# Loading the first pair's q and k into both partition halves, head by head on two queues, and making the router's constants later

## The chip, the cores and the metric

The kernel runs on one core of one Trainium2 chip. The metric is the device time of one execution in microseconds. A core has five engines that run their own instruction streams in order and wait for each other by semaphores: TensorE (PE, matmuls; PEld is its weight load), VectorE (DVE), ScalarE (ACT), GpSimd (POOL) and SyncE (SP), which here issues most of the DMAs; ScalarE can issue DMAs as well, from a queue of its own. Data lie in SBUF, in 128 partitions; TensorE writes to PSUM.

## What is computed

Attention over 8 batches and 8 heads with q pooled by two, then a mixture of experts with one expert for each of the 4608 rows:

```
q, k, v: (8, 8, 1152, 64) float32
q_pool = q.reshape(B, H, S // 2, 2, D).mean(axis=3)
scores = (1 / sqrt(D)) * q_pool @ k.transpose(0, 1, 3, 2)
attn   = softmax(scores)                 # row maximum subtracted
x      = (attn @ v) -> (4608, 512)
logits = x @ w_gate ; e = argmax(logits) ; gate = softmax(logits)[e]
out    = gate * sigmoid(x @ w_output_gate)[e] * (relu(x @ w1[e]) @ w2[e])
```

Everything is kept near float32 precision. A value is split into a high part (a cast to fp32r, or to fp16 for probabilities and v) and a low part (value minus high part), and a product is made of matmuls of these parts.

## The kernel before

**Pairs and tiles.** The heads are worked on in 32 pairs (one batch, two heads; `prep(n, table)` for pair n). A head has 64 dimensions, so a pair's q and k come as 128 partitions: head 0 in partitions 0 to 63, head 1 in 64 to 127. `qp` is q with its two rows to be pooled, `kpf` is k, `vp` is v. Matmuls need another layout: `ka[:, h]` holds head h's high part of k in both halves of the partitions, `qa` holds head h's high part of q in partitions 0 to 63 and its low part in 64 to 127, `kb` the low part of k and `qb` the high part of q in partitions 0 to 63; rows 64 to 67 of `kb` and `qb` carry constants and the row maxima. One matmul of `ka` with `qa` and one of `kb` with `qb` make three of the four products. `kp` (low part of k, both heads in their own halves) and `qd` serve the one query tile in which rows of both heads meet.

**How the layout is made.** `lk` loads q and k, two DMAs of 576 KB. `kh` casts k to `xk` (ACT), `qsum` adds the two rows of q (POOL), `qh` casts it to `xq` (ACT), `kl` and `ql` subtract for the low parts `kp` and `yq` (POOL), `qd` copies two corners (POOL). Then `dk`, `dq` and `dl` copy the parts from SBUF to SBUF into both halves: four DMAs for `ka`, two for `qa` and two for `qb` (from `xq`), two for `qa` and two for `kb` (from `yq` and `kp`). All twelve are issued by SP. `lv` loads v, `amax`, `gmax` and `scale` find its scale (ACT, a PE matmul over all partitions, DVE, POOL, DVE), and `vh`, `vs` and `vl` split it.

**Stages of a pair.** `mgen` makes the row maxima: 27 chunks for each pair, for each two or three matmuls into one of three PSUM banks (`mp`) and a reduction of DVE (`pm`). After the fifth query tile and after the last, `rows` transposes the maxima, DVE splits them into `mr`, and two small DMAs from ACT's queue (`qb<-mr`) write them into `qb`, rows 66 and 67. `scores` makes 18 steps of scores (`sps`), each with two exponentials on ACT and a subtraction on POOL or DVE; the second matmul of a step reads `qb`, so it needs the maxima. `av` multiplies by v, and `logits` and `router` choose the expert. After all pairs `Moe.run` does the experts.

**What sets the order.** PE, DVE, ACT and POOL run in the order in which the code records instructions. A table gives each step of `prep` a place in a grid of slots; the grid has 32 lead-in steps before the first score step. Pair 0 and pair 1 used `PREP0`, the others `PREP`. SP issues its DMAs in the recorded order as well. The DMAs of both queues share eight semaphores, so a DMA may also wait until the eighth before it has landed. `consts` makes the router's constants: it loads the router's weights (`wf`, 32 KB), splits them into `wgt` on ACT and DVE, and fills small tables on POOL; `init(0)` writes one row of zeros to memory and fills `di`. Both are recorded at lead-in step `1 - SLEAD + INIT`, so `INIT = 12` puts them 20 steps ahead of the first score step. The first matmul that reads `wgt` starts at 88.8 us.

Of the kernel before, what the change touches and what calls it, by code (L numbers as in the profile page):

```python
# [8 lines left out]
F32 = mybir.dt.float32  # L9
F32R = mybir.dt.float32r  # L10
# [5 lines left out]
ALU = mybir.AluOpType  # L16
# [7 lines left out]
PREP0 = ((0, 'lk'), (12, 'kh', 0), (13, 'kh', 1), (12, 'qsum'), (15, 'kl'), (18, 'dk', 0), (19, 'dk', 1), (21, 'qh'), (26, 'ql'), (26, 'dq', 0), (27, 'dq', 1), (29, 'qd'), (32, 'dl', 0), (33, 'dl', 1),  # L24
        (53, 'lv'), (71, 'amax', 0), (74, 'amax', 1), (81, 'gmax'), (82, 'scale', 0), (85, 'scale', 1), (90, 'scale', 2), (93, 'vh', 0), (93, 'vs', 0), (96, 'vh', 1), (97, 'vl', 0), (100, 'vs', 1), (104, 'vl', 1))
PREP = ((0, 'lk'), (12, 'kh', 0), (12, 'qsum'), (17, 'kh', 1), (18, 'kl'), (18, 'dk', 0), (19, 'dk', 1), (22, 'qh'), (24, 'dq', 0), (25, 'dq', 1), (26, 'ql'), (29, 'qd'), (30, 'dl', 0), (32, 'dl', 1),
        (63, 'lv'), (82, 'amax', 0), (88, 'amax', 1), (93, 'gmax'), (94, 'scale', 0), (95, 'scale', 1), (99, 'scale', 2), (100, 'vh', 0), (101, 'vs', 0), (103, 'vl', 0), (107, 'vh', 1), (107, 'vs', 1), (110, 'vl', 1))
BURST = {0: 2, 2: 2, 4: 2, 6: 2, 8: 1, 10: 2, 12: 2, 14: 2, 16: 3}
PLP = (1, 3, 7, 9, 13, 15)
PLPL = (1, 3, 5, 7, 9, 11, 13, 15, 17)  # L30
IMM = 0
INIT = 12
KPB = 2
ND = 18
NS = 3
# [27 lines left out]
def attention(tc, qT, kT, vL, wg, keep, xrows, idscr, cum, pairs, setup, scat, init):  # L63
    nc = tc.nc
    nb = len(pairs) // 4
    with ExitStack() as ctx:
        def pool(name, bufs=1, **kw):
            return ctx.enter_context(tc.tile_pool(name=name, bufs=bufs, **kw))
# [4 lines left out]
        ld = pool("a_ld")  # L73
        sq = pool("a_sq")
# [8 lines left out]
        def psum(hold=False, name="tp"):  # L83

            while len(held) == 3:
                pop() if fill else pendv.pop(0)()
            k = next(i for i in banks if i not in held)
            free(k)
            if hold:
                held.add(k)  # L90
            x = ps_m.tile([128, 512], F32, name=name, tag=f"mp{k}")
            return (x, k) if hold else x

        def free(k):
# [12 lines left out]
        QDs = [ep.tile([128, 128], F32R, name=f"qd{i}") for i in range(2)]  # L107
# [12 lines left out]
        def dmaf(o, i, q=nc.sync):  # L120
            q.dma_start(out=o.bitcast(F32), in_=i.bitcast(F32))

        def prep(n, table):

            p = pairs[n]
            b, hp = p
            ka, kb, qa, qb, vt = KAs[n % 3], KBs[n % 3], QAs[n % 3], QBs[n % 3], VTs[n % 2]
            sc = sm.tile([128, 2], F32, name="sc", bufs=4)
            states[n] = dict(ka=ka, kb=kb, qa=qa, qb=qb, vt=vt, sc=sc, p=p, n=n, qd=QDs[n % 2])
            kp = ld.tile([128, S], F32R, name=f"kp{n}", tag="kp", bufs=KPB)  # L130
            kpf = ld.tile([128, S], F32, name="kpf")
            states[n]['kp'] = kp
            qp = ld.tile([128, 2, NQ], F32, name="qp")
            vp = ld.tile([128, 2 * NC, 64], F32, name="vp")
            xk = sq.tile([128, S], F32R, name=f"xk{n}", tag="xk")
            yq = sq.tile([128, NQ], F32R, name="yq")
            qs = yq.bitcast(F32)
            xq = sq.tile([128, NQ], F32R, name="xq")
            am = sm.tile([128, 2], F32, name="am")
            ex = sm.tile([128, 2], U32, name="ex")  # L140
            inv2 = sm.tile([128, 2], F32, name="inv2")
            gm = []

            def lk():
                nc.sync.dma_start(out=qp, in_=qT[b, hp].rearrange("p (t n) -> p t n", t=2))
                nc.sync.dma_start(out=kpf, in_=kT[b, hp])

            def lv():
                nc.sync.dma_start(out=vp, in_=vL[b, hp].rearrange("p (c d) -> p c d", d=64))

            def kh(i):
                z = slice(i * NQ, i * NQ + NQ)
                nc.scalar.copy(out=xk[:, z], in_=kpf[:, z])

            def kl():
                nc.gpsimd.tensor_tensor(out=kp, in0=kpf, in1=xk.bitcast(F32), op=ALU.subtract)

            def qsum():
                nc.gpsimd.tensor_tensor(out=qs, in0=qp[:, 0], in1=qp[:, 1], op=ALU.add)

            def qh():
                nc.scalar.copy(out=xq, in_=qs)

            def ql():
                nc.gpsimd.tensor_tensor(out=yq, in0=qs, in1=xq.bitcast(F32), op=ALU.subtract)

            def qd():
                for h in range(2):
                    z = slice(64 * h, 64 * h + 64)
                    nc.gpsimd.tensor_copy(out=QDs[n % 2][z, z], in_=xq[z, 512 if h == 0 else 0:][:, 0:64])  # L170

            def dk(h):
                r = slice(64 * h, 64 * h + 64)
                dmaf(ka[0:64, h], xk[r])
                dmaf(ka[64:128, h], xk[r])

            def dq(h):
                r = slice(64 * h, 64 * h + 64)
                o = h * (NQ + 64)
                dmaf(qa[0:64, o:o + NQ], xq[r])  # L180
                dmaf(qb[0:64, h], xq[r])

            def dl(h):
                r = slice(64 * h, 64 * h + 64)
                o = h * (NQ + 64)
                dmaf(qa[64:128, o:o + NQ], yq[r])
                dmaf(kb[0:64, h], kp[r])

            def amax(h):
                j = sm.tile([128, NC, 64], F16, name="junk", bufs=1)  # L190
                nc.scalar.activation(out=j, in_=vp[:, NC * h:NC * h + NC], func=AF.Abs, scale=2.0 ** -17, accum_out=am[:, h:h + 1])

            def gmax():
                g, gk = psum(True)
                g = g[:, 0:2]
                nc.tensor.matmul(g, lhsT=onesf, rhs=am, start=True, stop=True)
                gm.extend((g, gk))

            def scale(i):
                if i == 0:  # L200
                    nc.vector.tensor_scalar(out=ex, in0=gm[0].bitcast(U32), scalar1=0x7F800000, scalar2=None, op0=ALU.bitwise_and)
                    free(gm[1])
                elif i == 1:
                    nc.gpsimd.tensor_scalar(out=inv2, in0=ex.bitcast(F32), scalar1=2.0 ** -100, scalar2=2.0 ** 3, op0=ALU.max, op1=ALU.mult)
                else:
                    nc.vector.reciprocal(out=sc, in_=inv2)

            def vh(h):
                nc.scalar.activation(out=vt[:, h, :, 0:64], in_=vp[:, NC * h:NC * h + NC], func=AF.Copy, scale=sc[:, h:h + 1])

            def vs(h):
                v = vp[:, NC * h:NC * h + NC]
                nc.gpsimd.tensor_scalar(out=v, in0=v, scalar1=sc[:, h:h + 1], scalar2=1.0, op0=ALU.mult, op1=ALU.mult)

            def vl(h):
                nc.gpsimd.tensor_tensor(out=vt[:, h, :, 66:130], in0=vp[:, NC * h:NC * h + NC], in1=vt[:, h, :, 0:64], op=ALU.subtract)

            P = functools.partial
            fns = dict(qd=qd, lk=lk, lv=lv, kh=kh, kl=kl, qsum=qsum, qh=qh, ql=ql, dk=dk, dq=dq, dl=dl, amax=amax, gmax=gmax, scale=scale, vh=vh, vs=vs, vl=vl)
            out = {}  # L220
# [338 lines left out]
        E = mybir.EngineType
        with tc.manual_schedule(engines={E.PE, E.DVE, E.Activation, E.Pool}):  # L560
            for s in range(-SLEAD, 0):
                for ph in range(3):
                    prep_at(s, ph)
                if s == -RI:
                    for i in (1, 2):
                        dmaf(QBs[i][64:66], QBs[0][64:66])
                        dmaf(KBs[i][64:68], KBs[0][64:68])
                if s == 1 - SLEAD + INIT:
                    consts()
# [7 lines left out]
            for s in range(18 * NP + 14):  # L577
# [531 lines left out]
```

## Time and profile before

| | |
|---|---|
| Time, median of 3 runs | 1570.87 us (1569.94 to 1573.25) |
| The profiled execution's own time | 1569.06 us |
| Its span, first to last instruction | 1567.4 us |
| Mean granted TensorE clock | 0.982 |
| Busy share of the span: PE, PEld, DVE, ACT, POOL | 95%, 89%, 69%, 69%, 63% |
| Bytes moved by DMA | 257.25 MB |

A profile row of the timeline has the start in us, the duration in us, the engine (SPq and ACTq are DMA issues), the source line, the operation, written and read tile and their shapes, the number of instructions merged, and in brackets the idle time of the engine before it and what ended it. A row of the windows has the stretch, its length, the busy time and the instructions of PE, PEld, DVE, ACT and POOL, the granted TensorE clock, the mean busy share of the DMA engines and the rate in GB/s. A row of the waits has who waited for whom, the total in us, how often, and the longest. A row of the groups has busy us and mean ns of one, then the idle time before them.

### The profile page before, as it was taken

What the parts mean: (1) busy time and instruction counts of PE and PEld (TensorE: products, weight loads), DVE (VectorE), ACT (ScalarE), POOL (GpSimd) and SP (SyncE); (2) the same over time, 40 slices, a digit from 0 to 9 for tenths busy, and PEclk for the clock granted to TensorE, in tenths of its full rate; (3) what the DMA queues carried; (4) which work ended last, traced back from release to release, by engine and by line L of the source; (5) the groups of instructions that cost most, each with busy time, mean ns of one, the idle gap of its engine ahead of it and who ended that gap; (6) DMA issues with size and microseconds to landing.
All of it is one profiled execution on the core that took longest, in us unless ns stands there. A gap on an engine that the chain in (4) does not pass through costs nothing. (4 is left out here: it accounts for less than half of the span.)

```text
span 1567.4 us, 41971 instructions
## 1 busy us (share of the span) xinstructions
PE 1491.5 (95%) x16438; PEld 1387.6 (89%) x16438; DVE 1078.0 (69%) x2256; ACT 1085.4 (69%) x1871; POOL 984.9 (63%) x908
## 2 busy tenths in 40 slices
PE   4999999999999999999999999879999999999985
PEld 3989999999999999999999999868989989989975
DVE  4667776777777777777777777567666666566564
ACT  2778888888888888888888888744445445445453
POOL 4778788879888889889888978634322323322200
PEclk9899999999999999999999999979999999999998
DMA  7756655675576466646756664246745666453640
GB/s 204 212 137 163 158 153 131 160 177 139 133 181 170 127 158 168 160 130 163 179 134 161 171 171 116 101 163 217 267 146 204 232 228 213 153 203 108 217 150 8
DMA packets 92980, 257.25 MB, mean 164 GB/s; under 512 B 12938, under 2 KB 17178, under 8 KB 92770
## 3 DMA queue, kind: packets, MB, share of 16 engines
q1 hardware_dynamic: 82474, 233.36, 52.3%
q0 software_dynamic: 9152, 20.85, 4.1%
q8 instruction: 133, 2.18, 0.6%
q14 instruction: 69, 0.57, 0.1%
q10 hardware_dynamic: 1152, 0.30, 0.1%
HBM read 164.23 MB, written 23.02 MB: 119 GB/s over the span
## 5 line engine op out<-in xcount | busy, mean ns | idle before, releaser
L255 DVE TENSOR_REDUCE pm<-mp 128x1 f32<-128x384 f32 x864 | 453.7, 550 | 226.9 <-PE mp L254 222.4
L333 POOL TENSOR_TENSOR pl<-p,ph 128x576 f16<-128x576 f32 x381 | 488.8, 1287 | 154.0 <-ACT ph L332 135.0
L254 PE MATMUL mp<-ka,qa 128*128 128x384 f32 x960 | 317.8, 347 | 20.2 <-DMA qa<-yq 18.9
L331 ACT ACTIVATE p<-sps 128x576 f32<-128x576 f32 x381 | 249.5, 655 | 99.9 <-PE sps L319 57.2
L346 PEld LDWEIGHTS <-ph 128*128 128x128 f16 x2880 | 262.7, 97 | 39.7 <-issue 30.6
L346 PE MATMUL av<-vt,ph 128*128 128x65 f16 x2880 | 295.9, 194 | 0.0
L347 PE MATMUL av<-vt,ph 128*128 128x64 f16 x2880 | 293.8, 194 | 0.0
L317 PE MATMUL sps<-qa,ka 128*128 128x288 f32 x1152 | 279.5, 324 | 14.6 <-DVE pl L327 8.4
L348 PE MATMUL av<-vt,pl 128*128 128x65 f16 x2880 | 293.0, 192 | 0.0
L347 PEld LDWEIGHTS <-ph 128*128 128x128 f16 x2880 | 265.7, 97 | 0.8
L348 PEld LDWEIGHTS <-pl 128*128 128x128 f16 x2880 | 266.0, 99 | 0.0
L254 PE MATMUL mp<-kb,qb 66*128 66x384 f32 x768 | 262.8, 342 | 0.6 <-DMA kb<-kp 0.6
L319 PE MATMUL sps<-qb,kb 68*128 68x288 f32 x1152 | 248.9, 298 | 4.7 <-DMA qb<-mr 4.7
L332 ACT ACTIVATE ph<-sps 128x576 f16<-128x576 f32 x381 | 247.6, 650 | 0.0
L317 PEld LDWEIGHTS sps<-qa,ka 128*128 128x128 f32 x1152 | 185.4, 192 | 19.5 <-DVE pl L327 9.3
L254 PEld LDWEIGHTS mp<-ka,qa 128*128 128x128 f32 x960 | 180.2, 192 | 22.9 <-issue 19.1
L319 PEld LDWEIGHTS sps<-qb,kb 68*128 68x128 f32 x1152 | 187.6, 191 | 5.1 <-issue 5.1
L831 ACT ACTIVATE hh<-hps 128x512 fp32r<-128x512 f32 x76 | 45.5, 598 | 191.3 <-PE hps L824 191.3
L824 PE MATMUL hps<-xh,w1h 128*128 128x256 f32 x608 | 173.3, 285 | 0.0
L824 PE MATMUL hps<-xl,w1h 128*128 128x256 f32 x608 | 173.1, 285 | 0.0
L824 PE MATMUL hps<-xh,w1l 128*128 128x256 f32 x608 | 172.6, 284 | 0.0
L327 DVE TENSOR_TENSOR pl<-sps,ph 128x576 f16<-128x576 f32 x195 | 146.6, 752 | 25.8 <-ACT sps L324 22.7
(208 smaller groups left out, 3154.8 us busy)
## 6 DMA issues: line engine op xcount, KB each, us to landing
ka<-xk SPq DMA_DIRECT2D x128, 288.0 KB
raw1b<-in_w_dram SPq DMA_DIRECT2D x24, 1024.0 KB
raw2b<-in_w_dram SPq DMA_DIRECT2D x24, 1024.0 KB
raw1a<-in_w_dram SPq DMA_DIRECT2D x22, 1024.0 KB
raw2a<-in_w_dram SPq DMA_DIRECT2D x22, 1024.0 KB
qp<-in_qT_dram SPq DMA_DIRECT2D x32, 576.0 KB
kpf<-in_kT_dram SPq DMA_DIRECT2D x32, 576.0 KB
vp<-in_vL_dram SPq DMA_DIRECT2D x32, 576.0 KB
```

The costliest lines, as they stand in the source:

```text
L254: nc.tensor.matmul(mp, lhsT=l, rhs=r, start=j == 0, stop=j == len(ops) - 1)
L255: nc.vector.tensor_reduce(out=pm[:, i:i + 1], in_=mp, axis=AX.X, op=ALU.max)
L317: nc.tensor.matmul(sps[:, j, 0:288], lhsT=ka[:, h, ks], rhs=qa[:, o + 288 * j:o + 288 * j + 288], start=True, stop=False)
L319: nc.tensor.matmul(sps[:, j, 0:288], lhsT=kb[:, h, ks], rhs=qb[:, h, 288 * j:288 * j + 288], start=False, stop=True)
L327: nc.vector.tensor_tensor(out=pl.rearrange("p (j n) -> p j n", j=2), in0=x, in1=ph2, op=ALU.subtract)
L331: nc.scalar.activation(out=p32.rearrange("p (j n) -> p j n", j=2), in_=x, func=AF.Exp, scale=1.0 / 16)
L332: nc.scalar.activation(out=ph2, in_=x, func=AF.Exp, scale=1.0 / 16)
L333: nc.gpsimd.tensor_tensor(out=pl, in0=p32, in1=ph, op=ALU.subtract)
L346: nc.tensor.matmul(av_[:, qb, 0:65], lhsT=hi, rhs=vt[:, h, c, 0:65], start=c == 0 and qb == 0, stop=False)
L347: nc.tensor.matmul(av_[:, qb, 0:64], lhsT=hi, rhs=vt[:, h, c, 66:130], start=False, stop=False)
L348: nc.tensor.matmul(av_[:, qb, 0:65], lhsT=lo, rhs=vt[:, h, c, 0:65], start=False, stop=c == NC - 1 and qb == 4)
L824: nc.tensor.matmul(hp[:, f], lhsT=W1[w][:, c, fs], rhs=d[x][:, c], start=i == 0, stop=i == 11)
```

## The change

Pair 0 gets a table of its own, `PREPF`, and steps of its own, which make the matmul layout without copies in SBUF. `lf(h)` loads head h's q and k twice each from memory, into partitions 0 to 63 and 64 to 127, head 0 from SP's queue and head 1 from ACT's: eight DMAs of 288 KB. `fq(h)` adds q's two rows in place (now DVE, all 128 partitions), casts the sum into `qa` (ACT) and copies a corner into `qd` (POOL). `fk(h)` casts k straight into `ka[:, h]` (ACT). `fl(h)` casts q into `qb` (ACT) and replaces the upper half of `qa` by the low part (DVE). `fb(h)` makes the low parts of k: `kb` for head 0 on DVE, `kp` for both heads and `kb` for head 1 on POOL. The second head's tiles are `kpx`, which takes a buffer of `kp`, and `vpx`, which takes the buffer of `vp`; `lv` of pair 0 is therefore recorded later. `INIT` goes from 12 to 27, which puts `consts` and `init(0)` 5 steps ahead of the first score step.

```diff
+PREPF = ((0, 'lf', 0), (1, 'lf', 1), (3, 'fq', 0), (4, 'fk', 0), (5, 'fl', 0), (6, 'fb', 0), (8, 'fk', 1), (54, 'fq', 1), (55, 'fb', 1), (60, 'fl', 1), (62, 'lv'),
+         (71, 'amax', 0), (74, 'amax', 1), (81, 'gmax'), ...
-INIT = 12
+INIT = 27
...
+            fs = [(kpf, qp)]
+            if table is PREPF:
+                fs.append((ld.tile([128, S], F32, name="kpx", tag="kp", bufs=KPB), ld.tile([128, 2, NQ], F32, name="vpx", tag="vp")))
+            def lf(h):
+                q_ = (nc.sync, nc.scalar)[h]
+                r = slice(64 * h, 64 * h + 64)
+                for z in (slice(0, 64), slice(64, 128)):
+                    q_.dma_start(out=fs[h][1][z], in_=qT[b, hp][r].rearrange("p (t n) -> p t n", t=2))
+                for z in (slice(0, 64), slice(64, 128)):
+                    q_.dma_start(out=fs[h][0][z], in_=kT[b, hp][r])
+            def fq(h):
+                a, b_ = fs[h][1][:, 0], fs[h][1][:, 1]
+                o = h * (NQ + 64)
+                z = slice(64 * h, 64 * h + 64)
+                nc.vector.tensor_tensor(out=a, in0=a, in1=b_, op=ALU.add)
+                nc.scalar.copy(out=qa[:, o:o + NQ], in_=a)
+                nc.gpsimd.tensor_copy(out=QDs[0][z, z], in_=qa[z, o + (512 if h == 0 else 0):][:, 0:64])
+            def fk(h):
+                nc.scalar.copy(out=ka[:, h], in_=fs[h][0])
+            def fl(h):
+                a = fs[h][1][:, 0]
+                o = h * (NQ + 64)
+                z = slice(64, 128)
+                nc.scalar.copy(out=qb[0:64, h], in_=a[0:64])
+                nc.vector.tensor_tensor(out=qa[z, o:o + NQ], in0=a[z], in1=qa.bitcast(F32)[z, o:o + NQ], op=ALU.subtract)
+            def fb(h):
+                k_ = fs[h][0]
+                z = slice(64 * h, 64 * h + 64)
+                if h == 0:
+                    nc.vector.tensor_tensor(out=kb[0:64, 0], in0=k_[0:64], in1=ka.bitcast(F32)[0:64, 0], op=ALU.subtract)
+                nc.gpsimd.tensor_tensor(out=kp[z], in0=k_[z], in1=ka.bitcast(F32)[z, h], op=ALU.subtract)
+                if h == 1:
+                    nc.gpsimd.tensor_tensor(out=kb[0:64, 1], in0=k_[0:64], in1=ka.bitcast(F32)[0:64, 1], op=ALU.subtract)
...
-                    preps[n] = prep(n, PREP if n > 1 else PREP0)
+                    preps[n] = prep(n, PREP if n > 1 else PREP0 if n else PREPF)
```

The order of the instructions moves at three places. Lines of the changed kernel stand 44 lower from `consts` on (L375, the load of `wf`, becomes L419). Numbers behind names are those of buffers.

First, SP's queue from the start of the program. Before, up to the first DMAs of pair 1:

```order
L145 DMA qp<-in_qT_dram 128x1152
L146 DMA kpf<-in_kT_dram 128x1152
L375 DMA wf<-in_wg_dram 128x64
L149 DMA vp<-in_vL_dram 128x1152
L121 DMA qb_128<-qb_127 2x1152
L121 DMA kb_119<-kb_118 4x2304
L121 DMA ka_121<-xk_157 64x1152 x4
L121 DMA qa_124<-xq 64x576
```

SP's queue now, from pair 0's load of v on (the four loads of `lf(0)`, three DMAs of constant rows and pair 1's q and k stand ahead of it):

```order
L193 DMA vp<-in_vL_dram 128x1152
L123 DMA ka_122<-xk_184 64x1152 x4
L123 DMA kb_117<-kb_118 4x2304
L123 DMA qa_125<-xq 64x576
L123 DMA qb_128<-xq 64x576
L123 DMA qa_125<-xq 64x576
L123 DMA qb_128<-xq 64x576
L123 DMA qa_125<-yq 64x576
L123 DMA kb_119<-kp_181 64x1152
L123 DMA qa_125<-yq 64x576
L123 DMA kb_119<-kp_181 64x1152
L419 DMA wf<-in_wg_dram 128x64
```

The load of `wf` moved from the third place to behind the twelve copies of pair 1, and pair 0's v moved behind pair 1's k.

Second, ACT. Before, from its first instruction to the first exponential:

```order
L153 ACT_TABLE_LOAD
L153 CAST xk_157<-kpf 128x576 x2
L162 CAST xq<-yq 128x576
L377 CAST wgt<-wf 128x4x16
L153 CAST xk_206<-kpf 128x576 x2
L191 ACTIVATE junk,am<-vp 128x576
L162 CAST xq<-yq 128x576
L191 ACTIVATE junk,am<-vp 128x576
L121 DMA qb_127<-mr 1x5x128 x2
L209 ACTIVATE vt_138<-vp,sc 128x9x64
L331 ACTIVATE p_363<-sps_358 128x576
```

ACT now, from its second cast of k (the DMAs of `lf(1)`, the table load and three casts of head 0 stand ahead):

```order
L164 CAST ka_121<-kpx 128x1152
L160 CAST qa_124<-vpx 128x576
L170 CAST qb_127<-vpx 64x576
L197 CAST xk_184<-kpf 128x576 x2
L235 ACTIVATE junk,am<-vp 128x576
L206 CAST xq<-yq 128x576
L235 ACTIVATE junk,am<-vp 128x576
L421 CAST wgt<-wf 128x4x16
L123 DMA qb_127<-mr 1x5x128 x2
L253 ACTIVATE vt_138<-vp,sc 128x9x64
L375 ACTIVATE p_365<-sps_360 128x576
```

The cast of `wgt`, which needs `wf`, moved from ahead of pair 1's casts to directly ahead of the DMAs of the row maxima.

Third, DVE, at the end of the first group of maxima. Before:

```order
L294 TENSOR_SCALAR mr<-tp 5x128
L295 SCALAR_TENSOR_TENSOR mr<-tp,mr 5x128
L255 TENSOR_REDUCE pm<-mp_327 128x1
L255 TENSOR_REDUCE pm<-mp_333 128x1
L255 TENSOR_REDUCE pm<-mp_337 128x1
L206 RECIPROCAL sc<-inv_162 128x2
```

and now:

```order
L338 TENSOR_SCALAR mr<-tp 5x128
L339 SCALAR_TENSOR_TENSOR mr<-tp,mr 5x128
L422 TENSOR_TENSOR wgt<-wf,wgt 128x4x16
L299 TENSOR_REDUCE pm<-mp_329 128x1
L299 TENSOR_REDUCE pm<-mp_335 128x1
L299 TENSOR_REDUCE pm<-mp_339 128x1
```

The subtraction for `wgt`, which stood ahead of all reductions, moved between the first group's maxima and the six reductions that come before the first scores.

More of the change, by code (lines that the diff above doesn't have):

```diff
@@ L27 @@
         (63, 'lv'), (82, 'amax', 0), (88, 'amax', 1), (93, 'gmax'), (94, 'scale', 0), (95, 'scale', 1), (99, 'scale', 2), (100, 'vh', 0), (101, 'vs', 0), (103, 'vl', 0), (107, 'vh', 1), (107, 'vs', 1), (110, 'vl', 1))
+PREPF = ((0, 'lf', 0), (1, 'lf', 1), (3, 'fq', 0), (4, 'fk', 0), (5, 'fl', 0), (6, 'fb', 0), (8, 'fk', 1), (54, 'fq', 1), (55, 'fb', 1), (60, 'fl', 1), (62, 'lv'),
+         (71, 'amax', 0), (74, 'amax', 1), (81, 'gmax'), (82, 'scale', 0), (85, 'scale', 1), (90, 'scale', 2), (93, 'vh', 0), (93, 'vs', 0), (96, 'vh', 1), (97, 'vl', 0), (100, 'vs', 1), (104, 'vl', 1))
 BURST = {0: 2, 2: 2, 4: 2, 6: 2, 8: 1, 10: 2, 12: 2, 14: 2, 16: 3}
@@ L133, in prep @@
             qp = ld.tile([128, 2, NQ], F32, name="qp")
-            vp = ld.tile([128, 2 * NC, 64], F32, name="vp")
             xk = sq.tile([128, S], F32R, name=f"xk{n}", tag="xk")
-            yq = sq.tile([128, NQ], F32R, name="yq")
-            qs = yq.bitcast(F32)
-            xq = sq.tile([128, NQ], F32R, name="xq")
             am = sm.tile([128, 2], F32, name="am")
@@ L142, in prep @@
             gm = []
+            fs = [(kpf, qp)]
[31 more added lines that the diff above has]
+                    nc.gpsimd.tensor_tensor(out=kb[0:64, 1], in0=k_[0:64], in1=ka.bitcast(F32)[0:64, 1], op=ALU.subtract)
+            vp = ld.tile([128, 2 * NC, 64], F32, name="vp", tag="vp")
+            if table is not PREPF:
+                yq = sq.tile([128, NQ], F32R, name="yq", tag="yq")
+                qs = yq.bitcast(F32)
+                xq = sq.tile([128, NQ], F32R, name="xq", tag="xq")
             def lk():
@@ L218, in prep @@
             P = functools.partial
-            fns = dict(qd=qd, lk=lk, lv=lv, kh=kh, kl=kl, qsum=qsum, qh=qh, ql=ql, dk=dk, dq=dq, dl=dl, amax=amax, gmax=gmax, scale=scale, vh=vh, vs=vs, vl=vl)
+            fns = dict(lf=lf, fq=fq, fk=fk, fl=fl, fb=fb, qd=qd, lk=lk, lv=lv, kh=kh, kl=kl, qsum=qsum, qh=qh, ql=ql, dk=dk, dq=dq, dl=dl, amax=amax, gmax=gmax, scale=scale, vh=vh, vs=vs, vl=vl)
             out = {}
```

## The prediction

> **What bounds the kernel now.** I read the page first, then TensorE's waits, then the first 60 us by engine. "B" is a time in the profiled execution before, "A" my estimate of the same event after.
>
> ```profile
> span 1567.4 us, 41971 instructions
> ...
> PE   4999999999999999999999999879999999999985
> ...
> PE mp L254 <- DMA qa<-yq: 18.9, 1, 18.9
> ...
> PE sps L319 <- DMA qb<-mr: 4.7, 2, 2.5
> ...
> 36.00:40.00 4.00, 3.77 (x14) 3.80 (x15) 1.14 (x3) 2.91 (x5) 1.64 (x2) 0.50 0.94 226
> 44.00:48.00 4.00, 4.00 (x16) 3.80 (x16) 2.75 (x6) 1.19 (x2) 1.97 (x2) 0.50 0.53 129
> 60.00:100.00 40.00, 39.06 (x518) 36.41 (x515) 29.17 (x70) 31.87 (x59) 31.40 (x29) 1.00 0.85 206
> ```
>
> After the first slice (39 us) TensorE is the bound: 39.06 of 40 us busy from 60 to 100. So whatever moves the first scores is carried to the end. Ahead of them lie two waits: 18.9 us for the first pair's operands, and up to 2.5 us for the row maxima (qb<-mr) at B 36.23. From 36 to 48 the granted clock is 0.50 although TensorE is full. The change reaches nothing later, so the sum is made over the first 42 us.
>
> **Loads and casts of the first head.**
>
> ```profile
> 0.80 1.28 ACT L153 ACT_TABLE_LOAD   x1 [0.80 <-PEq L1098]
> 6.86 1.24 ACT L153 CAST xk<-kpf 128x576 fp32r<-128x576 f32 x2 [4.77 <-DMA kpf<-in_kT_dram]
> ...
> 27.62 0.66 ACT L162 CAST xq<-yq 128x576 fp32r<-128x576 f32 x1
> ...
> 17.59 0.86 SPq L121 DMA_DIRECT2D kb<-kp  x1
> ...
> 20.14 0.66 PE L254 MATMUL mp<-kb,qb 66*128 66x384 f32 x1 [0.57 <-DMA kb<-kp]
> ...
> 0.00:2.00 2.00, 0.00 (x0) 0.00 (x0) 0.82 (x3) 1.20 (x1) 1.35 (x9) 1.00 0.17 25
> 2.00:4.00 2.00, 0.00 (x0) 0.00 (x0) 1.57 (x2) 0.09 (x1) 1.01 (x9) 1.00 0.88 288
> 4.00:6.00 2.00, 0.00 (x0) 0.00 (x0) 0.91 (x1) 0.00 (x0) 0.97 (x1) 1.00 1.01 364
> 16.00:18.00 2.00, 0.00 (x0) 0.00 (x0) 0.00 (x0) 0.00 (x0) 0.00 (x0) 1.00 1.02 237
> ...
> L796 DVE TENSOR_TENSOR w2l<-raw2a,w2h 128x1024 fp32r<-128x1024 f32 x44 | 54.0, 1227 | 15.2 <-ACT w2h L795 15.2
> ```
>
> Removed: the twelve SBUF copies of pair 0, the last issued at B 17.59, on which the first low-order matmul waits until B 20.14. Added: every byte of q and k is loaded twice, 2.36 MB instead of 1.18, to 64 partitions at a time. Before, 0.05 MB had moved by 2.0 us, 0.58 MB more by 4.0, then 364 GB/s: 1.18 MB by 5.5, and k was used at 6.86, so landing takes 1.3 us. What a load to 64 partitions costs no row shows. The ends are 364 GB/s (loads to 128 partitions) and 237 GB/s (copies to 64 partitions, DMA share 1.02). I take 237, because the destination is the same half; then k lands at A 2.0 + 2.31/0.237 + 1.3 = 13.1, and q, half the bytes, at 8.1. At 364 k lands at 9.7, 3.4 us earlier.
>
> The Trainium skill, "SBUF — State Buffer", sections "Door 1: The DMA port swizzle (why `[64,N]` ≈ `[32,N]`)" and "Can I just issue two DMAs to hit both halves?", says that partitions 0 to 63 reach only half of the DMA ports (196 GB/s at 1 MiB against 328) and that two DMAs to the two halves serialize, within 6%. By 196 to 218 GB/s k would land 0.9 to 2 us later than in the sum. The copies' 237 GB/s against the loads' 364 agree in kind.
>
> ScalarE's function table load now waits behind q (8.1 to 9.4), covered by k's landing at 13.1. Then the cast of k (1.24) ends at 14.3, the copy of q's rows into qb (0.66) at 15.0, and VectorE's subtraction of k, 1.227 x 1152/1024 = 1.38, at 15.7. The low-order matmul runs at A 15.8, 4.3 us ahead of B 20.14.
>
> **The second head, v and the maxima.**
>
> ```profile
> 20.84 8.37 DVE L255 TENSOR_REDUCE pm<-mp 128x1 f32<-128x384 f32 x15 [7.11 <-PE mp L254]
> ...
> 26.94 0.68 ACT L191 ACTIVATE junk<-vp 128x576 f16<-128x576 f32 x1
> 27.52 0.19 ACT L191 ACTIVATION_READ_ACCUMULATOR junk<-vp 128x1 f32 x1
> ...
> 27.11 2.65 POOL L156 TENSOR_TENSOR kp<-kpf,xk 128x1152 fp32r<-128x1152 f32 x1 [2.18 <-ACT xk L153]
> 29.73 1.42 POOL L165 TENSOR_TENSOR yq<-yq,xq 128x576 fp32r<-128x576 f32 x1
> ...
> 29.00 0.38 PE L196 MATMUL tp<-am,onesf 128*128 128x2 f32 x2 [0.40 <-ACT junk L191]
> ...
> 22.00:24.00 2.00, 2.00 (x8) 2.00 (x7) 1.71 (x4) 0.00 (x0) 0.49 (x1) 1.00 1.03 408
> 26.00:28.00 2.00, 2.00 (x11) 1.60 (x11) 1.98 (x5) 2.00 (x5) 0.89 (x1) 1.00 0.00 0
> 28.00:30.00 2.00, 1.60 (x10) 1.25 (x9) 1.64 (x6) 0.95 (x3) 2.00 (x2) 1.00 0.91 187
> ```
>
> VectorE does the fifteen reductions in one run, 0.56 us each, ending at B 29.21. Two operations of the second head now stand among them, 0.69 us each: they end at A 15.8 + 9.07 + 1.4 = 26.3. GpSimd has three subtractions where it had one, each 2.65: k's first half 14.3 to 17.0, its second half after the second q cast, 19.4 to 22.1, kb until 24.7; then pair 1's sum until 26.1, kp until 28.8, q's low part until 30.2 (B 31.15). kb is there before its matmuls at 26.3.
>
> v shares its buffer with the second q: its load, once the fourth of SyncE's queue, now waits for VectorE's second subtraction, A 20.8. A lone load costs 1.4 us to the first byte (issue at B 27.06, 0.37 MB moved from 28 to 30 at 237 GB/s means a start at 28.4), 0.59 MB at 408 GB/s, 1.3 to land: 4.1, so A 25.0. ScalarE needs 0.87 for the first half's maximum, then the q cast behind GpSimd's sum (26.1 to 26.75), then 0.87: the matmul of v's scale runs at A 27.6 against B 29.00. Still 1.4 us ahead.
>
> **The constants, where the gain is lost.**
>
> ```profile
> 27.06 3.47 SPq L121 DMA_DIRECT2D ka<-xk  x4
> ...
> 37.49 0.84 SPq L121 DMA_DIRECT2D kb<-kp  x1
> ...
> SPq L121 <- DMA qb<-mr: 1.2, 1, 1.2
> ...
> 13.23 0.24 ACT L377 CAST wgt<-wf 128x64 fp32r<-128x64 f32 x1 [4.55 <-POOL wgt L376]
> ...
> 31.13 2.33 ACTq L121 DMA_DIRECT2D qb<-mr  x2
> ...
> 36.23 0.82 PE L319 MATMUL sps<-qb,kb 68*128 68x288 f32 x2 [2.49 <-DMA qb<-mr]
> ```
>
> The router's weights (wf) were the third DMA of SyncE's queue. Now that DMA stands behind all twelve copies of pair 1, and the cast that reads it stands ahead of the two qb<-mr DMAs in ScalarE's queue. VectorE's subtraction of wgt stands behind that cast and ahead of six reductions; three of their matmuls fill the three PSUM banks, and the scores are queued behind them.
>
> When does wf land? Pair 1's k load waits for GpSimd at 17.0; with 4.1 it lands at 21.1, its casts end at 22.4, where B has 27.06. From there to the end of the twelfth copy's issue were 11.3 us before, 1.2 of it waiting for qb<-mr, which comes later now; one more small copy is put in between (0.65). So wf is issued at A 22.4 + 10.1 + 0.65 = 33.1. The copies' bytes, 2.65 MB at 237 GB/s from 23.8, last until 35.0, and wf lies behind them: landed at A 36.3. GpSimd's memset of wgt, four short operations behind its 30.2, is hidden by that.
>
> Then the cast 0.24, the two DMAs 2.33, and 2.77 until the scores' second matmul (36.23 - 33.46): A 41.65, 5.4 us after B 36.23. VectorE's six reductions (3.4 us from 36.8) end at 40.2, hidden behind it; so are GpSimd's other constants, which nothing of this stage reads.
>
> Sum: 1569.06 + 5.4 = 1574.5. The profiled execution was 1.8 us under the median of the three runs shown (1570.87), so for a median I say 1576. The sum leaves the second slow stretch of TensorE's clock as long as it was, since the same work stands at the same place.
>
> **Rivals.** Three of them use these rows: GpSimd's commonest subtraction, TensorE's matmuls where the first slow stretch ends, and the window in which the second one does.
>
> ```profile
> L333 POOL TENSOR_TENSOR pl<-p,ph 128x576 f16<-128x576 f32 x381 | 488.8, 1287 | 154.0 <-ACT ph L332 135.0
> ...
> 24.44 0.51 PE L254 MATMUL mp<-ka,qa 128*128 128x384 f32 x1
> 24.76 0.37 PE L254 MATMUL mp<-kb,qb 66*128 66x384 f32 x1
> 24.97 0.34 PE L254 MATMUL mp<-ka,qa 128*128 128x384 f32 x1
> ...
> 48.50:49.00 0.50, 0.50 (x4) 0.50 (x4) 0.06 (x1) 0.50 (x2) 0.00 (x0) 0.81 1.07 380
> ```
>
> 1. *The subtractions of VectorE and GpSimd can't run side by side.* GpSimd's first k subtraction then waits for VectorE's (1.38), which delays pair 1's load and all behind it; VectorE's second low part of q waits for GpSimd's 2.65, which puts v's load, 0.59 MB, in front of pair 1's copies. Together +2.7 beyond the sum: +8.1, 1579. Where GpSimd comes first, or also wins the next turn, some 1.5 more. For it: before, no two such operations met. Against: GpSimd's pl keeps its 1287 ns beside reductions, but these read PSUM. It decides at the first k cast, for which both wait. The Trainium skill, same page, section "Who interferes with whom", states it as a rule: a VectorE instruction with two SBUF inputs and a GpSimd instruction that reads SBUF exclude each other for the whole instruction. No row here shows it.
> 2. *Not slower: the loads to halves run at full rate.* Everything to wf moves 3.4 us forward: +2.0, 1573, inside the noise. It decides above 310 GB/s, where 2.3 us of the 5.4 are gone. For it: 364 and 408 GB/s when loading from memory; against: 237 to 64 partitions.
>
> 3. *Not slower: the clock.* TensorE was at half rate from B 36.2 until about 48.7, but after its first matmul at 18.9 only until 24.8, where a matmul's 0.51 turns into 0.34. If it recovers in 6 us, some 3.3 us (half of 12.5 - 6) come back: +2.1, 1573.
> 4. *The constants hold nobody up* (wf's bytes overtake, or are asked for sooner): the 1.4 us lead stays, 1569.5, or 4.8 with fast loads, 1566. The order of the queues speaks against it.
>
> **How the numbers follow.** About 0.2%, 3.1 us, can be told from no change. Chances: the sum 0.38, rival 1 0.30, rival 2 0.13, rival 3 0.12, rival 4 0.07. Slower: nearly all of the sum (0.36, since 5.4 is not far above that bound) and of rival 1, and a few of 2 and 3 that come with 1: 0.70. Faster: rival 4 with fast loads and what I overlooked, 0.07. The rest 0.23. The range goes from below rivals 2 and 3 (1571) to rival 1 where GpSimd also wins (1582).
>
> **What would show it.** DMA at about 240 GB/s from 2 to 12 us; the first low-order matmul near 16; the cast of wgt the longest ScalarE wait of the start, ended by wf at about 36, with TensorE idle some 7 us ahead of it; the scores' second matmul at 41 to 42. If the cast of wgt has no wait, the prediction is wrong in its sign. If VectorE's subtractions take more than 2 us or end with GpSimd's, rival 1 holds.

## The result: 0.76% slower

The changed kernel took 1582.04 us (median of 6 runs, 1579.04 to 1585.91), the kernel before 1570.8 us on the same chip (6 runs, 1569.55 to 1574.16): ratio 1.0076, 95% interval 1.0060 to 1.0092, 11.2 us slower between the medians and 11.9 by the ratio. The forecast was 1576 us, with a range of 1571 to 1582: the sign held, the loss is twice the one forecast, and the median lies just above the range. Lines from the router's constants on are 44 higher now than before (wgt's cast L377 is L421), those of the matmuls too (L254 is L298, L319 is L363).

The changed kernel: its span and TensorE's busy tenths in 40 slices, from the page; TensorE's waits (total, times, longest); and one row of VectorE's timeline.

```profile
span 1584.2 us, 41980 instructions
...
PE   3899999999999999999999999969999999999985
...
PE mp L298 <- ACT ka L164: 14.9, 1, 14.9
PE mp L298 <- DVE pm L299: 10.6, 5, 7.9
...
868.33 3.11 DVE L724 COPY cb<-cum 128x8 bf16<-128x8 bf16 x1
```

The first operands come 4.0 us earlier (14.9 after 18.9); the low-order matmul, for which 4.3 were forecast, comes 3.8 us earlier. In their place stand 10.6 us behind VectorE's reductions, 7.9 of them in one piece; before, no such wait in the first 48 us was over 0.2 us. The copy at 868.3 took 0.16 us in the kernel before. It took 3.1 us in four of the experiments as well (casts later with both kinds of loads, q's sum in PSUM, both of these), so it is not peculiar to the change. The profiled execution's own time, 1585.91, is 3.9 us over the median; the copy can be part of that, which is not shown. So the loss is read from the medians.

Timeline of the first head, on ScalarE, TensorE, GpSimd and VectorE (start, length, what ended the idle time before); then one window of 2 us while the loads run (last two columns: DMA share, GB/s).

```profile
8.58 1.28 ACT L160 ACT_TABLE_LOAD   x1 [8.58 <-DMA qp<-in_qT_dram]
13.69 1.15 ACT L164 CAST ka<-kpf 128x1152 fp32r<-128x1152 f32 x1 [3.14 <-DMA kpf<-in_kT_dram]
16.37 0.66 PE L298 MATMUL mp<-kb,qb 66*128 66x384 f32 x1 [0.79 <-DVE kb L177]
24.26 0.69 PE L298 MATMUL mp<-ka,qa 128*128 128x384 f32 x1 [2.10 <-DVE pm L299]
...
14.92 3.80 POOL L178 TENSOR_TENSOR kp<-kpf,ka 64x1152 fp32r<-64x1152 f32 x1 [3.50 <-ACT ka L164]
20.37 2.63 POOL L178 TENSOR_TENSOR kp<-kpx,ka 64x1152 fp32r<-64x1152 f32 x1
23.07 3.02 POOL L180 TENSOR_TENSOR kb<-kpx,ka 64x1152 fp32r<-64x1152 f32 x1
...
14.87 1.35 DVE L177 TENSOR_TENSOR kb<-kpf,ka 64x1152 fp32r<-64x1152 f32 x1 [3.54 <-ACT ka L164]
18.18 1.17 DVE L159 TENSOR_TENSOR vpx<-vpx 128x576 f32<-128x576 f32 x1
20.77 2.84 DVE L171 TENSOR_TENSOR qa<-vpx,qa 64x576 fp32r<-64x576 f32 x1
```

```profile
6.00:8.00 2.00, 0.00 (x0) 0.00 (x0) 0.00 (x0) 0.00 (x0) 0.00 (x0) 1.00 1.02 226
```

The loads run at 226 GB/s, k's cast starts at 13.69 and the low-order matmul at 16.37. But GpSimd's first subtraction takes 3.80 us where its twin for the second head takes 2.63, and VectorE's subtraction of the second q takes 2.84 us beside that twin; TensorE stalls 2.10 us at 24.26 for the latter.

The same timeline where the constants are, with the first matmul that reads wgt in the kernel before (L418) and now (L462); then three windows (third column from the right: granted clock).

```profile
18.75 0.34 SPq L190 DMA_DIRECT2D kpf<-in_kT_dram  x1
23.70 0.33 SPq L193 DMA_DIRECT2D vp<-in_vL_dram  x1
24.13 4.43 SPq L123 DMA_DIRECT2D ka<-xk  x4
35.92 0.59 SPq L419 DMA_DIRECT2D wf<-in_wg_dram  x1
37.95 0.42 SPq L190 DMA_DIRECT2D kpf<-in_kT_dram  x1
39.03 5.24 SPq L1117 DMA_DIRECT2D idscr<-di  x4
...
30.65 0.38 PE L240 MATMUL tp<-am,onesf 128*128 128x2 f32 x2 [0.74 <-ACT junk L235]
40.94 0.24 ACT L421 CAST wgt<-wf 128x64 fp32r<-128x64 f32 x1 [10.35 <-DMA wf<-in_wg_dram]
41.02 2.10 ACTq L123 DMA_DIRECT2D qb<-mr  x2
41.97 0.69 PE L298 MATMUL mp<-ka,qa 128*128 128x384 f32 x1 [7.86 <-DVE pm L299]
47.80 0.85 PE L363 MATMUL sps<-qb,kb 68*128 68x288 f32 x2 [3.07 <-DMA qb<-mr]
...
88.83 0.28 PE L418 MATMUL tp<-xh,wgt 128*128 128x256 f32 x1
100.43 0.28 PE L462 MATMUL tp<-xh,wgt 128*128 128x256 f32 x1
```

```profile
36.00:40.00 4.00, 0.00 (x0) 0.00 (x0) 0.00 (x0) 0.00 (x0) 0.00 (x0) 0.50 0.98 223
44.00:48.00 4.00, 0.93 (x4) 0.58 (x4) 0.77 (x2) 0.00 (x0) 0.75 (x1) 0.50 1.08 382
56.00:60.00 4.00, 4.00 (x16) 3.81 (x16) 2.75 (x7) 1.91 (x4) 1.57 (x2) 0.50 0.50 153
```

From 36 to 40 no compute engine does anything: all stand behind the load of wf. ScalarE waits 10.35 us for it, the maxima's DMAs (qb<-mr) go out at 41.02, land 4.7 us after their issue ends (2.77 before), and the scores' second matmul runs at 47.80 instead of 36.23: 11.6 us later, the whole loss. The first matmul that reads wgt, at 100.43 instead of 88.83, is still 11.6 us late.

### The profile page after: what moved, and what is told of

Its sections match the earlier page's. It is cut to its first block, busy times and chain, and to the rows that moved or that the text cites. A ratio compares the mean times of both kernels' runs of the same rounds, so it can differ in the third digit from the quotient of the medians.

```text
span 1584.2 us, 41980 instructions
## 1 busy us (share of the span) xinstructions
PE 1497.3 (95%) x16438; PEld 1391.0 (88%) x16438; DVE 1087.2 (69%) x2261; ACT 1087.7 (69%) x1874; POOL 992.0 (63%) x908
## 3 DMA queue, kind: packets, MB, share of 16 engines
q8 instruction: 133, 2.18, 0.6%
## 5 line engine op out<-in xcount | busy, mean ns | idle before, releaser
L377 POOL TENSOR_TENSOR pl<-p,ph 128x576 f16<-128x576 f32 x381 | 488.5, 1286 | 160.0 <-ACT ph L376 142.0
L298 PE MATMUL mp<-ka,qa 128*128 128x384 f32 x960 | 320.2, 350 | 26.4 <-ACT ka L164 14.9
L375 ACT ACTIVATE p<-sps 128x576 f32<-128x576 f32 x381 | 249.0, 654 | 101.2 <-PE sps L363 56.3
L298 PE MATMUL mp<-kb,qb 66*128 66x384 f32 x768 | 264.6, 345 | 0.8 <-DVE kb L177 0.8
L363 PE MATMUL sps<-qb,kb 68*128 68x288 f32 x1152 | 249.0, 298 | 4.6 <-DMA qb<-mr 4.6
L298 PEld LDWEIGHTS mp<-ka,qa 128*128 128x128 f32 x960 | 182.0, 194 | 29.6 <-ACT ka L164 14.9
L363 PEld LDWEIGHTS sps<-qb,kb 68*128 68x128 f32 x1152 | 187.6, 192 | 5.2 <-DMA qb<-mr 5.2
L371 DVE TENSOR_TENSOR pl<-sps,ph 128x576 f16<-128x576 f32 x195 | 146.6, 752 | 24.5 <-ACT sps L368 20.8
```

Of the source, the lines that this page charges most:

```text
L298: nc.tensor.matmul(mp, lhsT=l, rhs=r, start=j == 0, stop=j == len(ops) - 1)
L363: nc.tensor.matmul(sps[:, j, 0:288], lhsT=kb[:, h, ks], rhs=qb[:, h, 288 * j:288 * j + 288], start=False, stop=True)
L371: nc.vector.tensor_tensor(out=pl.rearrange("p (j n) -> p j n", j=2), in0=x, in1=ph2, op=ALU.subtract)
L375: nc.scalar.activation(out=p32.rearrange("p (j n) -> p j n", j=2), in_=x, func=AF.Exp, scale=1.0 / 16)
L377: nc.gpsimd.tensor_tensor(out=pl, in0=p32, in1=ph, op=ALU.subtract)
```

## The experiments

Two theories. **A**: the time goes into that one wait; the late load of wf holds its cast, and the cast holds the maxima's DMAs and VectorE's reductions. **B**: it goes into the new loads (half rate, subtractions that exclude each other, v later). Each kernel below was compared with the kernel before on the same chip. The events are those of the one profiled run (us); "us" is the ratio less one, times the median of before.

| kernel | ratio [95%] | us | first low-order matmul | v's scale | wgt's cast | scores' 2nd matmul | half rate until |
|---|---|---|---|---|---|---|---|
| before | 1 | 0 | 20.1 | 29.0 | 13.2 | 36.2 | 48.7 |
| changed | 1.0076 [1.0060, 1.0092] | +11.9 | 16.4 | 30.7 | 40.9 | 47.8 | 60.3 |
| constants later alone | 1.0084 [1.0068, 1.0101] | +13.1 | 19.5 | 29.8 | 41.8 | 48.0 | 58.2 |
| new loads alone | 1.0024 [1.0011, 1.0037] | +3.8 | 16.5 | 31.7 | 19.4 | 38.7 | 47.4 |
| wf early | 1.0008 [0.9993, 1.0023] | +1.3 | 16.5 | 30.2 | 32.9 | 37.0 | 41.1 |
| halves opposite | 1.0079 [1.0052, 1.0106] | +12.4 | 15.8 | 30.1 | 40.2 | 46.5 | 56.5 |
| casts later | 0.9999 [0.9984, 1.0014] | -0.2 | 16.7 | 30.8 | 47.8 | 37.1 | 41.0 |
| q's sum in PSUM | 1.0065 [1.0044, 1.0086] | +10.2 | 19.2 | 31.0 | 39.6 | 46.4 | 50.4 |
| both of these | 0.9991 [0.9978, 1.0004] | -1.4 | 19.3 | 31.0 | later | 36.7 | 46.9 |
| casts later, old loads | 0.9996 [0.9983, 1.0008] | -0.6 | 19.5 | 28.6 | later | 35.5 | 44.2 |
| second head in PSUM | 0.9998 [0.9982, 1.0013] | -0.3 | 16.4 | 27.8 | later | 34.6 | 38.3 |
| warm | 1.0004 [0.9991, 1.0016] | +0.6 | 16.5 | 27.9 | later | 34.5 | 38.5 |
| warm, old loads | 0.9995 [0.9981, 1.0009] | -0.8 | 19.2 | 27.9 | later | 35.0 | 47.7 |

The time follows the column of the scores' second matmul, and not the column of the first one.

**Constants later alone** (the kernel before, and `-INIT = 12` `+INIT = 27`).

> The kernel before with one edit, INIT = 27: the router's constants are made later, the loads and copies of the first pair stay as they were. Theory A (the late load of wf, which stops the cast of wgt and with it the row maxima's DMAs, is the main cause): wf is issued at about 38 us behind pair 1's copies, lands at about 40.5, the row maxima's DMAs go out at 41 instead of 31.1, the scores' second matmul runs at 46 to 47.5 instead of 36.2, and the time is 9.5 to 11 us above before: 1580 to 1582. Theory B (the new loads, the subtractions that get in each other's way and v's late load are the cause): nothing before 30 us changes, the time is that of before, 1571, within 2 us.

**New loads alone** (the changed kernel, and `-INIT = 27` `+INIT = 12`).

> The changed kernel with INIT back at 12: the new loads and steps of the first pair alone, wf loaded early, GpSimd's 2.3 us of constants between its first and its second head's work. Theory A: the matmul of v's scale comes 1.7 us later than before (30.65 against 29.0 in the changed kernel) and GpSimd's constants delay the second head by up to 2 more: 1573 to 1575. Theory B: as slow as the changed kernel, 1580 to 1583.

Waits in the timeline of constants later alone:

```profile
41.79 0.24 ACT L377 CAST wgt<-wf 128x64 fp32r<-128x64 f32 x1 [12.05 <-DMA wf<-in_wg_dram]
42.81 0.69 PE L254 MATMUL mp<-ka,qa 128*128 128x384 f32 x1 [9.24 <-DVE pm L255]
48.00 0.82 PE L319 MATMUL sps<-qb,kb 68*128 68x288 f32 x2 [2.42 <-DMA qb<-mr]
```

One number, with none of the first pair's loads touched, costs as much as the whole change (+13.1 us, somewhat more than theory A said), through the same wait on wf. The new loads with early constants cost 3.8 us, as theory A said. GpSimd's constants then stand between its first and its second head's subtraction, which starts at 22.51 (20.37 in the changed kernel), and TensorE stalls twice behind VectorE (1.93 and 2.10 us). How the 3.8 us divide between the loads and this place of the constants is not shown here; with the casts later, below, the loads cost nothing that can be told. The two parts do not add up to the change's 11.9 us; the likely reason is that there the second head's delay lies behind the wait for wf.

**wf early** (the changed kernel; only the load moves).

```
+                if s == 3 - SLEAD:
+                    nc.sync.dma_start(out=wf, in_=wg)
...
-            nc.sync.dma_start(out=wf, in_=wg)
```

> The changed kernel with one DMA moved: wf is loaded right behind the first head's loads, the rest of the constants stays late. Theory A: the cast of wgt waits only for GpSimd's memset (ends at 32.8) and stands at about 33 instead of 40.9, the row maxima's DMAs land at about 38 to 39, the scores' second matmul runs there instead of at 47.8: 1573 to 1574, 8 us under the changed kernel. Theory B: the cast moves but the scores still wait for something else after 44 us: 1580 to 1583.

```profile
5.85 0.37 SPq L612 DMA_DIRECT2D wf<-in_wg_dram  x1
...
32.93 0.24 ACT L420 CAST wgt<-wf 128x64 fp32r<-128x64 f32 x1 [2.74 <-POOL wgt L419]
37.00 0.50 PE L363 MATMUL sps<-qb,kb 68*128 68x288 f32 x2 [1.23 <-DMA qb<-mr]
```

Issued at 5.85, wf is there, and the cast waits only 2.74 us, for GpSimd's memset of wgt: 10.6 of the 11.9 us come back. The scores' second matmul runs at 37.00, earlier than the 38 to 39 of theory A.

**Halves opposite** (ScalarE's queue fills the upper half of the partitions first, while SyncE's fills the lower).

```
-                for z in (slice(0, 64), slice(64, 128)):
+                zs = (slice(0, 64), slice(64, 128))[::1 - 2 * h]
+                for z in zs:
...
```

> The changed kernel with the order of the halves turned round on ScalarE's queue alone: while SyncE's queue fills partitions 0 to 63, ScalarE's fills 64 to 127. Theory A1 (the rate of 225 GB/s from 2 to 12 us comes from both queues filling the same half at the same time): the loads run at 360 to 400 GB/s, k's first cast starts at 9 to 10 us instead of 13.7, and as the chain to wf starts there, the time falls by 3 to 4.5 us: 1578. Theory A2 (two DMAs to two halves serialize anyway): 225 to 240 GB/s, k's cast at 13 to 13.7, the time within 1.5 us of the changed kernel's 1582.

The five windows from 2 to 12 us moved 244, 219, 221, 253 and 235 GB/s, against 253, 224, 226, 217 and 226 in the changed kernel: 2% more on the mean. k's cast moved from 13.69 to 13.15. Loads to both halves at once share what one half gets. This is what the Trainium skill says ("SBUF — State Buffer", section "Can I just issue two DMAs to hit both halves?"), and the trace agrees. The time did not move.

**Casts later** (only ScalarE's cast into wgt and VectorE's subtraction move, from the constants to the seventh step of the main loop; the load of wf stays late), on the changed kernel and, as a control, on the old loads with late constants.

```
...
+                if s == 6:
+                    wcast()
```

> The changed kernel, with only the two casts of the router's weights (ScalarE's cast into wgt, VectorE's subtraction) recorded later, in the seventh step of the main loop; the load of wf and the other constants stay where the change put them. Theory A (the time is lost because the two casts stand in front of the maxima's DMAs and of the reductions, waiting for a late wf): the maxima's DMAs are issued at about 32, the scores' second matmul runs at 35.5 to 38 (47.8 in the changed kernel), and the time is that of the kernel before, ratio 0.999 to 1.001. Theory C (half of it is the traffic of the late constants and of pair 2's loads, which makes the maxima's DMAs land in 4 to 5 us instead of 2.8): ratio 1.002 to 1.004.

> The kernel before, with the constants at their later place but the two casts of the router's weights in the seventh step of the main loop. Theory A: nothing holds the maxima's DMAs any more, the scores' second matmul runs at 36 to 37 (48.0 with the constants late and the casts in line), ratio 0.999 to 1.001; beside the same edit on the changed kernel it tells what the new loads alone are worth (theory A: nothing that can be measured). Theory C: landing of the maxima's DMAs above 4 us, ratio 1.001 to 1.003.

Timeline of casts later, changed loads:

```profile
32.96 2.05 ACTq L123 DMA_DIRECT2D qb<-mr  x2
37.13 0.51 PE L363 MATMUL sps<-qb,kb 68*128 68x288 f32 x2 [1.56 <-DMA qb<-mr]
...
38.46 0.59 SPq L419 DMA_DIRECT2D wf<-in_wg_dram  x1
...
47.79 0.25 ACT L430 CAST wgt<-wf 128x64 fp32r<-128x64 f32 x1
```

wf is issued at 38.46, later than in the changed kernel, and its cast has no wait: the loss is gone (0.9999). Theory C fell with it: the maxima's DMAs land 2.1 us after their issue. That is theory A shown from its other side: not the late load costs, but what stands behind its reader. With the casts away, the old loads (0.9996) and the new ones (0.9999) give the same time.

**q's sum in PSUM**, alone and with the casts later (fq writes the sum to a PSUM tile, so that the subtraction in fl reads one operand from SBUF).

```
-                nc.vector.tensor_tensor(out=a, in0=a, in1=b_, op=ALU.add)
+                t = ps_s.tile([128, 2, 512], F32, name=f"qs{h}", tag=f"sps{h}")[:, :, 0:288]
...
+                nc.vector.tensor_tensor(out=t, in0=a..., in1=b_..., op=ALU.add)
...
```

> The changed kernel, with the sum of q's two parts written to PSUM, so that VectorE's subtraction of q reads one operand from SBUF and not two. Theory E (VectorE and GpSimd exclude each other when both read two operands from SBUF): the second head's subtraction takes 0.76 us beside GpSimd's 2.6 (2.84 in the changed kernel), and v's load is issued near 19.4 instead of 23.7, since only the sum still reads that buffer. Rival F (the 2.84 us are a wait for something else, as for ScalarE's copy): it stays over 2 us. For the time, theory A says that little comes back, since wf stays late: ratio to before 1.006 to 1.008; if the exclusion itself were the larger cost, 1.003 or less.

> The two edits together (casts of the router's weights later, q's sum in PSUM). Theory A with E: v's load is issued near 19.4, the matmul of v's scale runs at 28 to 29 (30.65 in the changed kernel, 29.0 before), the scores' second matmul at 34 to 36.3 (36.23 before), ratio 0.9985 to 1.0. If the first slow stretch of TensorE's clock or pair 1's own copies set the end, ratio 1.0 to 1.002.

VectorE and GpSimd with q's sum in PSUM:

```profile
15.74 0.76 DVE L173 TENSOR_TENSOR qa<-qs,qa 64x576 fp32r<-64x576 f32 x1 [7.65 <-ACT qb L172]
16.53 2.55 DVE L179 TENSOR_TENSOR kb<-kpf,ka 64x1152 fp32r<-64x1152 f32 x1
23.21 0.76 DVE L173 TENSOR_TENSOR qa<-qs,qa 64x576 fp32r<-64x576 f32 x1
...
15.26 2.61 POOL L180 TENSOR_TENSOR kp<-kpf,ka 64x1152 fp32r<-64x1152 f32 x1 [6.12 <-ACT ka L166]
22.79 2.65 POOL L180 TENSOR_TENSOR kp<-kpx,ka 64x1152 fp32r<-64x1152 f32 x1
```

The second subtraction takes 0.76 us beside GpSimd's 2.65, where it took 2.84: with one SBUF operand the two run together. The subtraction of k still reads two; it came second here, and now it is the longer one (2.55 against 1.35 in the changed kernel), while GpSimd's took 2.61 (3.80 there). So the first to start runs and the other waits until it is done. The Trainium skill states this ("SBUF — State Buffer", section "Who interferes with whom"), and these rows agree. Two things were not foreseen: VectorE's first subtraction waited for ScalarE's copy out of the same PSUM tile, and the first low-order matmul came at 19.2 instead of 16.4; and v's load, expected near 19.4, went out at 21.82, when VectorE's second sum was done. Yet v's scale (31.0 for 30.7) stayed where it was and the time was no worse (1.0065), so the 2.9 us at the first matmul did not reach either.

**Second head in PSUM, and warm.** Where does the lead of the loads go? Here only the second head's sum is in PSUM, the casts come later, and v's second maximum stands ahead of pair 1's cast of q. "Warm" adds matmuls of ones ahead of everything; the control has them (40 where warm has 34), and the casts later, on the old loads.

```
+        for _ in range(34):
+            nc.tensor.matmul(wu, lhsT=keep['ones'], rhs=<ones, 512 columns>, start=True, stop=True)
```

> The changed kernel with three edits: the casts of the router's weights later (seventh step of the main loop); the second head's sum of q in PSUM, the first head's left in SBUF; the maximum of v's second half taken ahead of pair 1's cast of q on ScalarE. Question: where does the four-microsecond lead of the new loads go once the constants hold nobody? Theory S (into the 2.1 us stall of TensorE behind VectorE's 2.84 us subtraction, and into the half-rate clock, which lasts until TensorE has run some microseconds without a gap): the first low-order matmul at 16.4 to 16.8, no stall of 2 us, full rate (384 columns each 0.18 us) by 24 instead of 31, the matmul of v's scale at 26 to 28.5, the scores' second matmul at 32 to 35, ratio 0.997 to 0.999. Theory G (GpSimd's three subtractions bind, whatever TensorE does): TensorE waits for GpSimd's kb instead, the matmul of v's scale at 29 to 31, ratio 0.9995 to 1.001.

> The same as the kernel with the second head's sum in PSUM, and ahead of everything 34 matmuls of ones by ones (bf16, 512 columns, result unused), which keep TensorE busy from about 2 us while the loads run. Theory W (the first tiles run at half rate only because TensorE was idle until then): the tiles run 0.18 us apart or at VectorE's 0.56 us per reduction from 16.5 on, fifteen reductions end by 26.5, the scores' second matmul at 31 to 34, ratio 0.996 to 0.998. If earlier work doesn't matter for the clock, the first tiles stay at 0.32 us per matmul and the ratio is that of the kernel without these matmuls.

> The kernel before with late constants and the casts of the router's weights in the seventh step of the main loop, and 40 matmuls of ones by ones ahead of everything. It tells what the new loads are worth when the clock is out of the way. VectorE's fifteen reductions (9.2 us from the first low-order matmul at 19.5) bound the first tiles already, so theory W expects the matmul of v's scale at 28 to 29 and the scores' second matmul at 34.5 to 35.5, ratio 0.9985 to 1.0, 1 to 4 us more than the same matmuls ahead of the new loads.

TensorE in the second head in PSUM (last of these rows: the first matmul that reads wgt), then in warm; last, one window of warm:

```profile
27.83 0.41 PE L247 MATMUL tp<-am,onesf 128*128 128x2 f32 x2
28.37 0.34 PE L305 MATMUL mp<-kb,qb 66*128 66x384 f32 x1
34.57 0.51 PE L370 MATMUL sps<-qb,kb 68*128 68x288 f32 x2 [1.83 <-DMA qb<-mr]
84.68 0.28 PE L471 MATMUL tp<-xh,wgt 128*128 128x256 f32 x1
...
1.12 9.11 PE L602 MATMUL tp<-ones 128*128 128x512 bf16 x34 [1.12 <-DVE ones L679]
15.04 0.69 PE L305 MATMUL mp<-ka,qa 128*128 128x384 f32 x1 [4.81 <-ACT ka L170]
16.98 0.52 PE L305 MATMUL mp<-ka,qa 128*128 128x384 f32 x1
...
15.00:16.00 1.00, 0.69 (x1) 0.28 (x1) 0.98 (x1) 1.00 (x2) 0.93 (x1) 0.50 0.00 0
```

The events came as theory S said (v's scale at 27.8, scores at 34.6, 1.7 us ahead of before), but full rate came only at 28.1, not by 24, and the time did not move. The interval alone doesn't explain that. The 1.7 us are inside it, but the first matmul that reads wgt ran at 84.68, 4.15 us ahead of 88.83, and the interval's end, 0.9982, allows a gain of 2.8. Either that lead is lost later or this execution (1562.44, 3.6 us under its median) is not typical; this stays open. The warm-up was lost again in the 4.8 us of idle time before the first tile, which theory W had not counted on, so whether a warm TensorE would help is not decided. No version beats the kernel before by more than its interval.

## Why the prediction was right in sign and half in size

Right, by its own steps: the loads to halves (217 to 253 GB/s, taken as 237), k's cast (13.69; 13.1 was said), the low-order matmul (16.37; 15.8), the queue behind wf as the cause, the cast of wgt as ScalarE's longest wait, and TensorE's idle time ahead of it (7.86; some 7). Rival 2 (full rate) and rival 4 fell. Rival 3 (sooner clock) did not happen: half rate lasted 12.5 us after the scores' second matmul before, and 12.5 now (47.8 to 60.3). In five experiments it did (wf early, casts later, q's sum in PSUM, second head in PSUM, warm: 3.8 to 4.1 us), and its price was too high. From the scores' second matmul to the first that reads wgt these took 49.6 to 50.2 us, before and changed 52.6: some 8.5 us less of half rate gave 2.4 to 3.0 us, where the rival counted half.

Wrong were three terms of the sum, which put that matmul at 41.65; it ran at 47.80, 6.15 later:

1. *wf's issue, 33.1 forecast, 35.92 measured (+2.8).* The step that failed is GpSimd's "each 2.65" and "two operations of the second head, 0.69 us each": the subtractions took 3.80, 2.63 and 3.02 us, and VectorE's two operations 1.17 and 2.84. This is rival 1, shown by q's sum in PSUM. Pair 1's k load stands behind GpSimd's first subtraction and was issued at 18.75 (17.0 said), 1.15 us of it from that subtraction's length. So pair 1's copies began at 24.13 (22.4 said), and issuing the twelve took 11.8 us where 10.75 were counted. v's load waited for VectorE until 23.70 (20.8 said), directly ahead of these copies. That the exclusion is the whole of the 2.8 is not shown: in PSUM wf was issued at 36.20, while GpSimd's subtractions for the second head, with pair 1's behind them, began 2.4 us later (22.79 for 20.37). With the second head's sum alone in PSUM v's load was issued at 19.43, but the copies began at 23.78, only 0.7 us ahead of casts later, so VectorE's 2.84 us did little to their start.
2. *wf's cast, 3.2 us after that issue forecast, 5.0 measured (+1.8).* Its bytes lie behind copies that fill the DMA (share 0.98 from 36 to 40), which the forecast had done by 35.0. v's 0.59 MB just ahead of them could account for it: where v was loaded earlier, the same stretch was 3.4 us (q's sum in PSUM) and 3.5 (constants later alone), in halves opposite, where v was as late, 4.7. It was not isolated.
3. *The maxima's landing, 2.77 forecast, 4.68 measured (+1.9).* The sum took it over from before. But what stood behind wf in SyncE's queue, pair 2's loads (37.55, 37.95) and four writes of idscr (39.03), now ran at the same time: 382 GB/s from 44 to 48. In the four kernels whose cast waits for a late wf it was 4.0 to 4.7, in the others at most 2.8. Which of the two transfers does it was not separated.

Their sum is 6.5; cast and issue together took 2.18 us where 2.57 were counted, which gives 0.4 back. Rival 1 (0.30) is what happened, but its price, +2.7, is about the first term alone; the second and third, 3.7 us together, add up at the same wait. That the time came out at the upper end of rival 1 (1582) is luck: that end was set for a GpSimd that also wins the next turn, and it did not, since VectorE's 2.84 us ended at 23.61 and GpSimd's next subtraction took 3.02.

Two premises were also too simple. "Whatever moves the first scores is carried to the end" held for the loss, but not for the lead of the second head in PSUM, as far as the times show. And "4.3 us ahead" at the first matmul is no lead to spend. With q's sum in PSUM, with or without the casts later, that matmul was 2.9 us later than in the changed kernel, and v's scale at the same 31.0.

## What to carry to other kernels

Before moving setup work "later", list for each engine what its queue holds behind the instruction that reads the late data, and put that reader (not the load) past the critical items: the same late load cost 12 us or nothing. When a transfer is delayed, ask which transfers come after it in its queue, since they move onto the next critical small DMA. A lead at the start counts only at the last event that the steady stage waits for; follow it there before booking it.

## What the runs showed of the hardware

Half rate of TensorE came in steps. Windows of 1 us at the ends of such a stretch, in before (two rows) and in wf early (two rows):

```profile
35.00:36.00 1.00, 0.00 (x0) 0.00 (x0) 0.00 (x0) 0.00 (x0) 0.14 (x1) 0.52 0.34 72
48.00:49.00 1.00, 1.00 (x6) 1.00 (x6) 0.56 (x1) 0.83 (x2) 0.00 (x0) 0.65 1.00 365
...
37.00:38.00 1.00, 1.00 (x6) 1.00 (x7) 0.05 (x1) 0.46 (x1) 0.00 (x0) 0.83 0.11 28
41.00:42.00 1.00, 0.95 (x6) 0.66 (x6) 0.86 (x2) 0.85 (x2) 1.00 (x2) 0.96 1.16 199
```

A mean of 0.52 in a window means half rate in 0.96 of it, so before ran at half rate from 35.04 to 48.70, 13.66 us; wf early from 37.66 to 41.08, 3.42 us. The other profiled runs give 3.4 (casts later, second head, warm), 6.8 (new loads alone, casts later on old loads), 13.7 (both of these, warm on old loads), 17.1 (q's sum in PSUM), 23.9 (halves opposite) and 27.3 us (changed, constants alone): 1, 2, 4, 5, 7 and 8 times 3.41. The Trainium skill ("TensorE: Matmul & The Clock Gate", section "What's actually happening") gives a window of 3413 ns, and these lengths agree. It also puts full rate after at least one busy window; here one was not always enough: from 36.23 to 48.70 TensorE had no idle time, over three windows. Why some runs need one and others nearly four is open. Short idle times were enough to lose it: in before TensorE's last matmul ended at 33.75 and half rate began 1.3 us later; in wf early it began at 37.66, after only 1.23 us of idle time that had ended at 37.00.

In the first tiles the granted clock's column reads 1.00 although matmuls of 384 columns stand 0.32 us apart (0.18 later): it shows nothing before the first change, as warm tells, where the same pace reads 0.50. With the new loads full rate came at 28 to 31, with the old ones at 24 to 27. A rule that gaps of TensorE start the count again is not borne out: after the last gap of over 0.5 us it took 3.9 us in new loads alone and 10.7 in q's sum in PSUM.
